# Windowed attention and a folded gated FFN in one kernel: attention by blocks of 128 queries, a new order of the work

## The chip, the core and the metric

The kernel runs on one core of a Trainium2 chip. The metric is the time of one execution on the device in microseconds; several executions are timed and the median counts. Lower is better.

## The reference

For 4 batches of 8 heads, 768 positions and head size 64, attention with four sink keys and a window of 128; its output, with the heads side by side, is the input of a gated feed-forward part.

```python
scores = scale * np.matmul(q, k.transpose(0, 1, 3, 2))
keep = is_sink | in_window           # pos < 4, or 0 <= q_pos - k_pos < 128
a = softmax(np.where(keep, scores, -1e9))
x = np.matmul(a, v)                  # -> [3072, 512]
h = (x @ w1) * (x @ w2) @ w3         # 512 -> 1024 -> 1024
out = h @ w_out                      # 1024 -> 512
```

## The kernel before, in words

All matmuls are in bf16. Since nothing nonlinear stands between them, w3 and w_out are folded into one matrix `w3o` at the start (`fold_w3` transposes rows of w3, `fold_mm` multiplies them with w_out). So each batch has these stages.

- **Keys and queries.** `load_qkv` loads k, q and v of a block of 128 positions on POOL's queue, converting to bf16. For batches 0 and 1, PE transposes them (`transposes`, tile `tp`) and VectorE copies them to `kqT`; for batches 2 and 3, SP issues DMA transposes (`transposes_dma`, one for k and one for q of a block).
- **Scores.** A pair of heads r is two matmul chains on the two halves of PE's rows (64 each, the head size). A score unit fills one PSUM tile `sc`; ScalarE takes the exponential (`ex`), VectorE multiplies with the mask (`am`). Most units are made by `scores(b, r, t)`: one pair of heads, a tile t of 256 queries, so four units for each of the three tiles of a batch. The tiles (0, 0) and (0, 1) (`BLOCKS`) are made by `block_scores(b, j, r0, r1)`: a block j of 128 queries and two pairs of heads (all four for j = 0, which has no earlier block). The two PSUM buffers of `sc` allow two units in flight. The keys at the sink are done by `sink_scores` (tile `sp`).
- **Values.** `values` or `block_values` multiply `am` with v (tile `av`), VectorE divides by the sums (`rec`, `xn`). `xn` is transposed to `xT` by PE (tile `xt`) or, for batches 1 to 3, by DMA on SP's queue (`x_transposes_dma`).
- **Gates.** `gate` makes x @ w1 and x @ w2 for a chunk of 256 or 384 tokens (tile `pg`); ScalarE copies one, VectorE multiplies the other with it into `ab`.
- **Output.** `project` multiplies `ab` with `w3o` for 128 tokens (tile `po`); ScalarE copies to SBUF, and SP sends the 256 KB out.

The order on every engine is made at build time. Each piece of work is a `task` with a priority, with its stages (engine and an assumed duration), with what must be done before (`after`), which loads it needs (`loads`), and what must have been started before (`started`). `landings` works out when loads are assumed to arrive, and `plan` then goes through assumed time: PE takes the task that can start first, and among those that can start at once the one with the lowest number (`prio`, changed for single tasks by `nudge`). `paced` tasks, the scores, are also held until ScalarE's backlog is small and until a given time after the scores before (`PACE`). `lead` marks the first of two score units that are to follow each other on PE; it waits for two free PSUM buffers. The engines then run what the plan wrote down, each in its order, and semaphores alone decide when.

At the start, `raws` lists nine transfers of 512 KB of w3 and w_out in fp32 that SP issues at once; ScalarE, VectorE or both convert them (`cast`). POOL waits for the raw transfer with the number `hold` (a copy to `spent`) and then begins its own loads in the order `order`. Where PE would stand still in the first 40 us, `keep_busy` puts in dummy matmuls (tile `pz`).

Of the kernel before, what the change touches and what calls it, by code (L numbers as in the profile page):

```python
# [21 lines left out]
def kernel(  # L22
# [13 lines left out]
    nc = tc.nc  # L36
    FP32 = mybir.dt.float32
# [89 lines left out]
    def load(what, *i):  # L127
# [9 lines left out]
        else:  # L137
# [13 lines left out]
    nudge = {("g", 0, 2, 6, 0): -300, ("g", 1, 2, 4, 0): -1200, ("g", 0, 1, 3, 1): 60, ("fm", 6, 3): 1500}  # L151
# [94 lines left out]
    def segments(t):  # L246
        segs = [] if t == 0 else [(2 * t - 1, 2 * t, P, 0)]
        return segs + [(2 * t, 2 * t, 2 * P, P), (2 * t + 1, 2 * t + 1, P, 3 * P)]

    ams = {}  # L250

    def scores(b, r, t):
        c0 = P if t == 0 else 0
        sc = ps_sc.tile([P, 2, 512], FP32, tag="sc", name="sc")
        for i, (kb, qb, n, c) in enumerate(segments(t)):
            for e in range(2):
                hp = slice(64 * e, 64 * e + 64)
                nc.tensor.matmul(sc[:, e, c:c + n], kT[b][hp, r, kb * P:(kb + 1) * P],  # L258
                                 qT[b][hp, r, qb * P:qb * P + n],
                                 start=True, stop=True)  # L260
        yield
        ex = work.tile([P, 2, 512], BF16, tag="ex", name="ex")
        nc.scalar.activation(ex[:, :, c0:], sc[:, :, c0:], ACTF.Exp, scale=scale)  # L263
        yield
        am = work.tile([P, 2, 512], BF16, tag="am", bufs=4, name="am")
        mk = maskt[:, min(t, 1):min(t, 1) + 1, c0:].to_broadcast([P, 2, 512 - c0])
        nc.vector.tensor_mul(am[:, :, c0:], ex[:, :, c0:], mk)  # L267
        ams[b, r, t] = am
        yield
# [52 lines left out]
    def block_x_transposes(b, j):  # L322

        t, i = j // 2, j % 2
        xt = ps_mm.tile([P, NP, P], BF16, tag="mm", name="xt")
        for r in range(NP):
            nc.tensor.transpose(xt[:, r, :], xns[b, t][:, i, r, :, :].rearrange("p e d -> p (e d)"), ident)
        yield
        nc.scalar.copy(xT[b][:, :, j * P:(j + 1) * P], xt[:])
        yield  # L330

    def values(b, r, t):

        am = ams.pop((b, r, t))
        av = ps_mm.tile([P, 2, 2, D + 1], FP32, tag="mm", name="av")
        todo = []
        for i in range(2):
            if t > 0:
                q0 = (t - 1) * 256 + i * P
                todo.append((av[:, i, :, :].rearrange("p e d -> p (e d)"), es[b][:, q0:q0 + P],  # L340
                             vs[b][:, 2 * r:2 * r + 2, :].rearrange("p e d -> p (e d)")))
            for kb, c in ((2 * t + i - 1, 2 * i * P), (2 * t + i, (2 * i + 1) * P)):
                if kb >= 0:
                    for e in range(2):
                        todo.append((av[:, i, e, :], am[:, e, c:c + P],
                                     vN[b][:, kb, 2 * r + e, 0:D + 1]))
        for n, (o, lhs, rhs) in enumerate(todo):
            nc.tensor.matmul(o, lhs, rhs, start=(n == 0), stop=(n == len(todo) - 1),  # L348
                             skip_group_check=True)
        yield  # L350
        rec = work.tile([P, 2, 2, 1], FP32, tag="rec", name="rec")
        nc.vector.reciprocal(rec[:], av[:, :, :, D:D + 1])  # L352
        if r == 0:
            xns[b, t] = work.tile([P, 2, NP, 2, D], BF16, tag="xn", bufs=3, name="xn")
        nc.vector.tensor_mul(xns[b, t][:, :, r, :, :], av[:, :, :, 0:D],  # L355
                             rec[:].to_broadcast([P, 2, 2, D]))
        yield

    def x_transposes(b, r0, t):

        xt = ps_mm.tile([P, 2, 2, P], BF16, tag="mm", name="xt")
        for r in range(2):
            for i in range(2):
                nc.tensor.transpose(xt[:, r, i, :],
                                    xns[b, t][:, i, r0 + r, :, :].rearrange("p e d -> p (e d)"),
                                    ident)
        yield
        nc.scalar.copy(xT[b][:, r0:r0 + 2, t * 256:(t + 1) * 256],
                       xt[:].rearrange("p r i m -> p r (i m)"))
        yield  # L370
# [74 lines left out]
    def project(b, m, n0, n1):  # L445
# [10 lines left out]
        (nc.scalar if n0 > DM // 2 else nc.sync).dma_start(out=out[t0:t0 + P, n0:n1], in_=o_sb)  # L456
# [22 lines left out]
    def landings(taken, RAW=2.0, POOL=3.0, DGE=1.3, RAMP=(0.75, 1.0)):  # L479
# [3 lines left out]
        taken, owed = sorted((t + 4.0, us) for t, us in taken), 0.0  # L483
# [3 lines left out]
        while any(at[n] < len(q) for n, q in queues.items()):  # L487
# [8 lines left out]
            while taken and taken[0][0] <= now:  # L496
                owed += taken.pop(0)[1]
            if owed > 0.0:
                owed -= 0.02
                now += 0.02  # L500
                continue
# [3 lines left out]
            for n in busy:  # L505
# [35 lines left out]
    for i in range(KFF):  # L541
# [7 lines left out]
        for h, (j0, j1) in enumerate(FM[i]):  # L549
# [11 lines left out]
            if last and (i % 2 or i >= 4):  # L561
                tasks["fm", i, h]["frees"] = ("fm", i if i >= 4 else i - 1, 0)
    unit = []
    last_av = []
    for b in range(B):
        for t in range(NT):
# [17 lines left out]
            else:  # L584
                if b not in SINKS:
                    task(("ss", b, t), -1, sink_scores(b, t, t + 1), [("pe", 0.12), ("act", 0.4)],
                         qk + [("sk", b)], ring="mm", started=[] if (b, t) in BLOCKS else [("sc", b, 1, t)])
                elif t == 1:
                    more = [(n, b, kb) for n in (("tdk", "tdq") if (b, 2) in XPOSE else ("tpk",)) for kb in (4, 5)]
                    task(("ss", b, 1), -1, sink_scores(b, 1, NT), [("pe", 0.225), ("act", 0.6)],  # L590
                         qk + more + [("sk", b)], ring="mm", started=[("sc", b, 1, 1)])
            if (b, t) in BLOCKS:
                parts = [(j, r0, r0 + 2, [2 * i + r0 // 2]) for i, j in enumerate(kbs) for r0 in (0, 2)]
                if t == 0:
                    parts = [(0, 0, NP, [0, 1])] + parts[2:]
                for u, (j, r0, r1, avs) in enumerate(parts):
                    task(("sc", b, u, t), 4, block_scores(b, j, r0, r1),
                         [("pe", 0.23), ("act", 1.05), ("dve", 0.7)],
                         [("tpk", b, kb) for kb in (j - 1, j) if kb >= 0], ring="sc", paced=True,
                         started=([unit[-1][0]] if unit else []) + (unit[-4][1] if len(unit) > 3 else []))  # L600
                    for a in avs:
                        task(("av", b, a, t), 3, block_values(b, j, 2 * (a % 2)),
                             [("pe", 0.125 if j == 0 else 0.245 if j == 1 else 0.36), ("dve", 0.55)],
                             [("sc", b, u, t)] + ([("ss", b, 1 if b in SINKS else t), ("sv", b)] if t else []),
                             [("v", b, j)], "mm", last_av)
                        last_av = [("av", b, a, t)]
                    unit.append((("sc", b, u, t), [("av", b, a, t) for a in avs]))
                    if avs[-1] % 2:
                        task(("xt", b, 2 * (j % 2), t), 2.5, block_x_transposes(b, j),
                             [("pe", 0.225), ("act", 0.6)],  # L610
                             [("av", b, avs[-1] - 1, t), ("av", b, avs[-1], t)], [], "mm")
                continue
            for r in range(NP):
                after = list(qk)
                if b >= 2 and t == 0:
                    after += [("g", b - 2, len(CHUNKS[b - 2]) - 1, dt, 1) for dt in range(KFF)]
                lead = r % 2 == 0
                task(("sc", b, r, t), 4 if lead else 0, scores(b, r, t),
                     [("pe", 0.17), ("act", 0.83), ("dve", 0.58)] if t == 0 else
                     [("pe", 0.225), ("act", 1.05), ("dve", 0.7)], after, ring="sc",  # L620
                     slots=2 if lead else 1, paced=lead,
# [215 lines left out]
```

## Time and profile before

| | |
|---|---|
| timed runs | 196.29, 197.38, 197.56 us; median 197.38 |
| profiled execution | 196.08 us, of which the span of its instructions 194.4 us |
| PE, PEld busy | 188.2 and 123.7 us |
| VectorE, ScalarE, POOL busy | 114.4, 103.9 and 75.6 us |
| granted TensorE clock | 1.00 |
| DMA | 29.17 MB, mean 150 GB/s |

A busy time is the sum over an engine's instructions, and a share is that against the span. PE (the matmuls) and PEld (their weight loads) overlap each other. Matmuls are pipelined: the time from one start to the next is what a matmul costs in a row of them, not its own duration. The time of an execution has some 1.7 us around the span.

### The profile page before, as it was taken

The page shows a single profiled execution, that of the slowest core. Times are in us where ns is not written, and L with a number is a line of the kernel's source. Part 1 is how long each engine was busy: PE and PEld are TensorE (multiplying, and loading weights), DVE is VectorE, ACT ScalarE, POOL GpSimd, SP SyncE. Part 2 cuts the span into 40 slices and gives each one's busy share as a digit, 9 for nine tenths or more (in the row PEclk, how much of TensorE's full clock was granted, in tenths as well). Part 3 has the DMA queues.
Part 4 walks back from the last instruction along what each step waited for, and adds up shares of the span by engine and source line. Part 5 has one row for each costly group of instructions (what it writes and reads, how often), then busy time and mean ns, then how long its engine had stood idle before and what let it go on. Part 6 is the DMA issues. An engine that isn't in the chain of part 4 may idle for free.

```text
span 194.4 us, 4625 instructions
## 1 busy us (share of the span) xinstructions
PE 188.2 (97%) x1830; PEld 123.7 (64%) x1830; DVE 114.4 (59%) x277; ACT 103.9 (53%) x177; POOL 75.6 (39%) x102
## 2 busy tenths in 40 slices
PE   7899799999999999999999999999999999999993
PEld 2346376998867786788788455556666666644443
DVE  5465588755699987967678036778886434410000
ACT  3515369743866876566574376567773333333232
POOL 5199967689999944433364330000000000000000
PEclk9999999999999999999999999999999999999999
DMA  5999999999999999999999999999320200014334
GB/s 209 414 380 159 184 165 197 193 158 154 156 152 192 198 146 125 154 157 187 118 154 142 142 157 220 211 217 120 78 56 2 55 0 0 0 55 164 146 133 153
DMA packets 107589, 29.17 MB, mean 150 GB/s; under 512 B 98608, under 2 KB 103088, under 8 KB 107568
## 3 DMA queue, kind: packets, MB, share of 16 engines
q0 software_dynamic: 79520, 12.33, 90.5%
q1 hardware_dynamic: 27904, 16.49, 40.1%
q8 instruction: 14, 0.23, 0.5%
q10 hardware_dynamic: 144, 0.07, 0.1%
q14 instruction: 7, 0.06, 0.1%
HBM read 29.39 MB, written 6.29 MB: 184 GB/s over the span
## 4 chain that ended last, share of the span: by engine, by line
PE 82%; DMA 11%; POOL 3%; SPq 2%; issue 0%; DVE 0%; ACT 0%; DVEq 0%
PE pg L388 39%; PE po L449 21%; PE av L348 6%; PE sc L258 5%; DMA kqT<-qN 4%; DMA ab<-in_moe_w_dram 4%; DMA qN<-in_q_dram 3%; PE tp L211 3%; PE pw L435 2%; PE av L311 1%; PE sc L279 1%; SPq L375 1%; PE ph L435 1%; SPq L163 1%; PE sp L240 1%; POOL qN L108 1%
## 5 line engine op out<-in xcount | busy, mean ns | idle before, releaser
L388 PE MATMUL pg<-xT,w_sb 128*128 128x256 bf16 (+1 forms) x640 | 91.0, 294 | 0.0
L388 PEld LDWEIGHTS <-w_sb 128*128 128x128 bf16 x640 | 59.5, 98 | 20.1 <-issue 1.1
L395 ACT COPY a_sb<-pg 128x256 f32<-128x256 f32 (+1 forms) x80 | 33.3, 416 | 37.0 <-PE pg L388 22.5
L392 DVE TENSOR_TENSOR ab<-a_sb,pg 128x256 bf16<-128x256 f32 (+1 forms) x80 | 37.7, 472 | 24.8 <-PE pg L388 22.8
L449 PE MATMUL po<-w3o,ab 128*128 128x512 bf16 (+2 forms) x208 | 43.0, 363 | 0.0
L263 ACT ACTIVATE ex<-sc 128x1024 bf16<-128x1024 f32 (+1 forms) x40 | 37.6, 962 | 6.5 <-PE sc L258 5.9
L449 PEld LDWEIGHTS <-ab 128*128 128x128 bf16 x208 | 19.3, 98 | 20.4 <-issue 0.2
L267 DVE TENSOR_TENSOR am<-ex,maskt 128x1024 bf16<-128x1024 bf16 (+1 forms) x40 | 25.3, 646 | 9.9 <-ACT ex L263 9.9
L453 ACT COPY w_sb<-po 128x512 f32<-128x512 f32 (+2 forms) x25 | 14.1, 566 | 25.9 <-PE po L449 25.8
L108 POOL DMA_DIRECT2D vN<-in_v_dram x24 | 21.6, 902 | 12.9 <-DMA kN<-in_k_dram 9.9
L108 POOL DMA_DIRECT2D qN<-in_q_dram x24 | 22.1, 919 | 9.9 <-DMA vN<-in_v_dram 6.2
L108 POOL DMA_DIRECT2D kN<-in_k_dram x24 | 22.0, 918 | 7.7 <-DMA qN<-in_q_dram 5.4
L355 DVE TENSOR_TENSOR xn<-av,rec 128x256 bf16<-128x256 f32 x40 | 17.0, 425 | 1.4
L348 PE MATMUL av<-vN,am 128*128 128x65 bf16 x296 | 16.7, 193 | 0.0
L348 PEld LDWEIGHTS <-am 128*128 128x128 bf16 x296 | 14.5, 97 | 1.8 <-DVE rec L352 0.2
L258 PE MATMUL sc<-kqT 64*128 64x128 bf16 (+1 forms) x216 | 11.8, 238 | 0.2 <-DMA kqT<-qN 0.2
L453 DVE COPY w_sb<-po 128x128 f32<-128x128 f32 x1 | 0.3, 292 | 19.7 <-ACT w_sb L453 19.7
L348 PE MATMUL av<-vs,es 128*128 128x130 bf16 x56 | 11.0, 220 | 0.0
L213 DVE COPY kqT<-tp 128x1024 bf16<-128x1024 bf16 x12 | 8.3, 689 | 4.6 <-PE tp L211 4.4
L352 DVE RECIPROCAL rec<-av 128x4 f32<-128x4 f32 x40 | 7.1, 178 | 5.9 <-PE av L348 5.5
L258 PEld LDWEIGHTS <-kqT 64*128 64x128 bf16 x216 | 7.0, 94 | 4.6 <-issue 4.0
L283 ACT ACTIVATE ex<-sc 128x1024 bf16<-128x1024 f32 x7 | 7.2, 1026 | 4.2 <-PE sc L279 4.2
(71 smaller groups left out, 140.5 us busy)
## 6 DMA issues: line engine op xcount, KB each, us to landing
out_dram<-w_sb SPq DMA_DIRECT2D x23, 256.0 KB
kN<-in_k_dram POOLq DMA_DIRECT2D x24, 128.0 KB, 8.4
qN<-in_q_dram POOLq DMA_DIRECT2D x24, 128.0 KB, 8.2
vN<-in_v_dram POOLq DMA_DIRECT2D x24, 128.0 KB, 8.0
w_sb<-in_moe_w_dram POOLq DMA_DIRECT2D x9, 256.0 KB, 8.3
ab<-in_moe_w_out_dram SPq DMA_DIRECT2D x3, 512.0 KB
ab<-in_moe_w_dram SPq DMA_DIRECT2D x3, 512.0 KB
kN<-in_moe_w_out_dram SPq DMA_DIRECT2D x1, 512.0 KB
```

What stands on the lines that cost most here:

```text
L108: nc.gpsimd.dma_start(out=dst, in_=rows(src, b, kb))
L213: nc.vector.tensor_copy(kqT[b][:, :, :, kb * P:(kb + 1) * P], tp[:])
L258: nc.tensor.matmul(sc[:, e, c:c + n], kT[b][hp, r, kb * P:(kb + 1) * P], qT[b][hp, r, qb * P:qb * P + n], start=True, stop=True)
L263: nc.scalar.activation(ex[:, :, c0:], sc[:, :, c0:], ACTF.Exp, scale=scale)
L267: nc.vector.tensor_mul(am[:, :, c0:], ex[:, :, c0:], mk)
L348: nc.tensor.matmul(o, lhs, rhs, start=(n == 0), stop=(n == len(todo) - 1), skip_group_check=True)
L355: nc.vector.tensor_mul(xns[b, t][:, :, r, :, :], av[:, :, :, 0:D], rec[:].to_broadcast([P, 2, 2, D]))
L388: nc.tensor.matmul(pg[:], w_sb[:, kk, dt * P:(dt + 1) * P], xT[b][:, kk, tk], start=(kk == 0), stop=(kk == NP - 1))
L392: nc.vector.tensor_mul(ab[b][:, dt, tk], gate_a.pop((b, c, dt))[:], pg[:])
L395: nc.scalar.copy(a_sb[:], pg[:])
L449: nc.tensor.matmul(po[:], ab[b][:, kk, m * P:(m + 1) * P], w3o[:, kk, n0:n1], start=(kk == 0), stop=(kk == KFF - 1))
L453: (nc.vector.tensor_copy if n0 == DM // 2 else nc.scalar.copy)(o_sb, po[:])
```

## The change

Every batch is now done by `block_scores` and `block_values`; `scores`, `values`, `x_transposes`, `segments` and `BLOCKS` are gone. `UNITS` lists all 44 score units in order of batch and block (one for block 0 of a batch, two for each later one). They are paired one after the other along this list, also across blocks and batches, except those in `SINGLE`. A unit waits for the transposed keys of its own blocks (`keys`), the leading one for those of its partner too, no longer for a whole tile. DMA transposes of `xn` are tasks for each block, when its own values are done.

The raw transfers come in another order and are converted by other engines, and POOL waits for the fourth of them (`hold = 4`). `landings` no longer takes the transposes' share away piece by piece, but assumes 2.1 us in place of 0.845 for a load from block 2 of batch 2 on, and a delay that grows; a DMA transpose is assumed to be done after 9.2, 6.0 or 3.0 us, not 8.4, 5.0 or 2.7. `nudge` and `PACE` hold other numbers, the sinks' priority is 0.5 and not -1. Three output tiles (`HALVED`) are sent as two DMAs each.

```diff
-    BLOCKS = ((0, 0), (0, 1))
+    UNITS = [(b, j, r0, NP if j == 0 else r0 + 2) for b in range(B) for j in range(NB) for r0 in ((0,) if j == 0 else (0, 2))]
+    SINGLE = ((0, 0), (3, 0))
+    HALVED = ((3, 1), (3, 2), (3, 3))
...
-    raws = [("wo", 2, 4, "act"), ("w3", 4, 5, "act"), ("w3", 0, 1, "both"), ("wo", 0, 2, "dve"),
-            ("w3", 1, 2, "dve"), ("wo", 4, 6, "dve"), ("wo", 6, 8, "dve"), ("w3", 2, 3, "both"),
-            ("w3", 3, 4, "act")]
-    hold = 5
+    raws = [("wo", 0, 2, "dve"), ("w3", 0, 1, "dve"), ("w3", 4, 5, "dve"), ("wo", 2, 4, "act"),
+            ("w3", 2, 3, "both"), ("w3", 3, 4, "act"), ("wo", 4, 6, "both"), ("wo", 6, 8, "act"),
+            ("w3", 1, 2, "act")]
+    hold = 4
...
-    nudge = {("g", 0, 2, 6, 0): -300, ("g", 1, 2, 4, 0): -1200, ("g", 0, 1, 3, 1): 60, ("fm", 6, 3): 1500}
+    nudge = {("g", 0, 1, 2, 0): -300, ("g", 1, 0, 2, 1): 60, ("p", 3, 5, 256): -60, ("av", 3, 1, 1): 1500,
+             ("tpk", 1, 5): 3, ("g", 1, 0, 2, 0): -60, ("xt", 0, 0, 2): -3, ("g", 1, 1, 0, 1): 60}
...
-        (nc.scalar if n0 > DM // 2 else nc.sync).dma_start(out=out[t0:t0 + P, n0:n1], in_=o_sb)
+        step = DM // 2 if (b, m) in HALVED else n1 - n0
+        for c in range(n0, n1, step):
+            (nc.scalar if n0 > DM // 2 else nc.sync).dma_start(out=out[t0:t0 + P, c:c + step],
+                                                               in_=o_sb[:, c - n0:c - n0 + step])
...
-            return [(0.95 if i[0] == 0 else 0.87, 0.845, [(x, i[0], kb)])
+            return [(0.95 if i[0] == 0 else 0.87, 0.845 if 6 * i[0] + kb < 14 else 2.1, [(x, i[0], kb)])
...
-                        arrive[key] = now + lag + min(2.5, max(0.0, 0.25 * (now - 36.0)))
+                        arrive[key] = now + lag + min(2.5, max(0.0, 0.25 * (now - 36.0))) + min(3.0, max(0.0, 0.1 * (now - 70.0)))
...
+    roles, partner, lead = {}, {}, None
+    for n, (b, j, r0, _) in enumerate(UNITS):
+        if lead is None and (b, j) not in SINGLE and n + 1 < len(UNITS):
+            roles[b, j, r0], partner[b, j, r0] = "lead", UNITS[n + 1][:2]
+            lead = b, j, r0
+        else:
+            roles[b, j, r0] = "more" if lead else "single"
+            lead = None
...
+                after = keys(b, j) + (keys(*partner[b, j, r0]) if role == "lead" else [])
...
+                if avs[-1] % 2:
+                    both = [("av", b, 2 * i, t), ("av", b, 2 * i + 1, t)]
+                    if (b, t) in X_XPOSE:
+                        task(("xd", b, t, i), 1, x_transposes_dma(b, t, i), [("sp", 1.3), ("dma", 1.2)], both)
...
-    PACE = [[0, 1.3, 0], [0, 0, 0], [6.2, 0, 0], [5.3, 0, 0]]
+    PACE = [[0, 0, 0], [5.8, 3.9, 0], [0, 0, 0], [0, 0, 0]]
...
-                    done[k["name"]] = at + (8.4 if at < end - 4.0 else 5.0 if at < end else 2.7)
+                    done[k["name"]] = at + (9.2 if at < end - 4.0 else 6.0 if at < end else 3.0)
```

How the order changes is seen at three places.

**PE, scores of block 1 of batch 0**, before (L279 is `block_scores`, L435 `fold_mm`, L311 `block_values`):

```order
L435 MATMUL ph_296<-wo_sb_81,w3t_354 128x512
L279 LDWEIGHTS kqT_0_95
L279 MATMUL sc_380<-kqT_0_95 128x128
...
L311 MATMUL av_393<-vN_0_91,am_375 128x65
...
L405 MATMUL tp3_409<-ident_73,w3_sb_80 128x128
...
L279 MATMUL sc_418<-kqT_0_95 128x128
```
and now (L259 is `block_scores`, L291 `block_values`, L345 `fold_w3`):

```order
L291 MATMUL av_389<-vN_0_91,am_377 128x65
L259 LDWEIGHTS kqT_0_95
L259 MATMUL sc_395<-kqT_0_95 128x128
...
L259 MATMUL sc_408<-kqT_0_95 128x128
...
L345 LDWEIGHTS w3_sb_80
L345 MATMUL tp3_419<-ident_73,w3_sb_80 128x128
```
Two units of eight matmuls (`sc_380`, `sc_418`) stood apart, with folds and values between them; now the two (`sc_395`, `sc_408`) follow each other without anything between.

**SP, the transposes of batch 2's last blocks** (`kqT_2`, L218, of loaded k and q) among those of `xn` (L375), before:

```order
L218 DMA_TRANSPOSE kqT_2_97<-kN_2_89 128x4x128
L375 DMA_TRANSPOSE xT_1_100<-xn_1528 128x4x128 x2
L218 DMA_TRANSPOSE kqT_2_97<-qN_2_85 128x4x128
...
L375 DMA_TRANSPOSE xT_2_101<-xn_1685 128x4x128 x2
...
L218 DMA_TRANSPOSE kqT_3_98<-kN_3_90 128x4x128
```
and now (L221 and L315):

```order
L315 DMA_TRANSPOSE xT_1_100<-xn_1540 128x4x128
L315 DMA_TRANSPOSE xT_2_101<-xn_1709 128x4x128
L221 DMA_TRANSPOSE kqT_2_97<-kN_2_89 128x4x128
L221 DMA_TRANSPOSE kqT_2_97<-qN_2_85 128x4x128
...
L315 DMA_TRANSPOSE xT_2_101<-xn_1709 128x4x128
L221 DMA_TRANSPOSE kqT_2_97<-qN_2_85 128x4x128
L315 DMA_TRANSPOSE xT_2_101<-xn_1958 128x4x128
```
The transposes of `xn` stood in twos, and both halves of a tile went when the tile's last values were done. Now they stand singly among those of k and q. The last row but one is q of block 5 of batch 2; ahead of it stands the `xT` transpose of block 1 of that batch.

**VectorE, the start**, before (L410 copies transposed rows of w3, L415 converts raw weights):

```order
L410 COPY kN_1_88<-tp3_203 128x512
L410 COPY kN_1_88<-tp3_208 128x512
L415 CAST w3_sb_80<-ab_0_103 128x512
L415 CAST wo_sb_81<-ab_1_104 128x1024
L410 COPY w3t_231<-tp3_220 128x512
```
and now (L350 and L355):

```order
L355 CAST wo_sb_81<-ab_0_103 128x1024
L355 CAST w3_sb_80<-ab_0_103 128x1024
L350 COPY w3t_212<-tp3_202 128x512
L350 COPY w3t_212<-tp3_207 128x512
L355 CAST w3_sb_80<-ab_0_103 128x1024
L350 COPY kN_1_88<-tp3_223 128x512
```
The first two raw transfers were converted by ScalarE before; now the first three are converted by VectorE, and the first rows that PE transposes come from its second conversion.

More of the change, by code (lines that the diff above doesn't have):

```diff
@@ L244, in sink_scores @@
         yield
-    def segments(t):
-        segs = [] if t == 0 else [(2 * t - 1, 2 * t, P, 0)]
-        return segs + [(2 * t, 2 * t, 2 * P, P), (2 * t + 1, 2 * t + 1, P, 3 * P)]
     ams = {}
[L252 to L269, printed above, removed]
     def block_scores(b, j, r0, r1):
@@ L329, in block_x_transposes @@
         nc.scalar.copy(xT[b][:, :, j * P:(j + 1) * P], xt[:])
[L330 to L369, printed above, removed]
         yield
@@ L591 @@
                          qk + more + [("sk", b)], ring="mm", started=[("sc", b, 1, 1)])
[L592 to L612, printed above, removed]
@@ L613 @@
[L613 to L614 removed]
+            for b_, j, r0, r1 in UNITS:
+                if (b_, j // 2) != (b, t):
+                    continue
+                u, i = (j % 2) * 2 + r0 // 2 - (j == 1), j % 2
+                avs = [0, 1] if j == 0 else [2 * i + r0 // 2]
+                role = roles[b, j, r0]
+                after = keys(b, j) + (keys(*partner[b, j, r0]) if role == "lead" else [])
                 if b >= 2 and t == 0:
                     after += [("g", b - 2, len(CHUNKS[b - 2]) - 1, dt, 1) for dt in range(KFF)]
[L617 to L621, printed above, removed]
[L622 to L632 removed]
@@ L633 @@
-            if (b, t) in X_XPOSE:
-                for i in range(2):
-                    task(("xd", b, t, i), 1, x_transposes_dma(b, t, i), [("sp", 1.3), ("dma", 1.2)],
-                         [("av", b, NP - 1, t)])
+                task(("sc", b, u, t), 0 if role == "more" else 4, block_scores(b, j, r0, r1),
+                     [("pe", 0.23), ("act", 1.05), ("dve", 0.7)], after, ring="sc",
+                     slots=2 if role == "lead" else 1, paced=role != "more",
+                     started=([unit[-1][0]] if unit else [])
+                     + (unit[-3 if role == "lead" else -4][1] if len(unit) > 3 else []))
@@ new lines @@
+                for a in avs:
+                    task(("av", b, a, t), 3, block_values(b, j, 2 * (a % 2)),
+                         [("pe", 0.125 if j == 0 else 0.245 if j == 1 else 0.36), ("dve", 0.55)],
+                         [("sc", b, u, t)] + ([("ss", b, 1 if b in SINKS else t), ("sv", b)] if t else []),
+                         [("v", b, j)], "mm", last_av)
+                    last_av = [("av", b, a, t)]
+                unit.append((("sc", b, u, t), [("av", b, a, t) for a in avs]))
@@ L796, in plan @@
             advance(k, free[e])
-        return taken
-    taken = []
-    for last in (False, False, True):
-        landings(taken)
-        taken = plan(last)
+    landings()
+    plan(True)
 _INS = ['q', 'k', 'v', 'n_sink', 'window', 'moe_w1', 'moe_w2', 'moe_w3', 'moe_w_out']
```

35 lines of the change are left out of this document (10 added, 25 removed).

## The prediction

> **What bounds the kernel now.** I read the page first, then PE's own waits, then the chain of waits at the two places where PE stood still, then SP's and POOL's queues there.
>
> ```profile
> span 194.4 us, 4625 instructions
> PE 188.2 (97%) x1830; PEld 123.7 (64%) x1830; DVE 114.4 (59%) x277; ACT 103.9 (53%) x177; POOL 75.6 (39%) x102
> PE 82%; DMA 11%; POOL 3%; SPq 2%; issue 0%; DVE 0%; ACT 0%; DVEq 0%
> ```
> TensorE is busy 97% of the span, ScalarE and VectorE little over half. The chain that ends last is PE for 82%, and a transfer for 11%. So a change gains by taking work off PE or by ending one of PE's waits. These are PE's waits, all of them:
>
> ```profile
> PE pz L463 <- DVE ksbd L172: 1.3, 1, 1.3
> PE tp L211 <- DMA qN<-in_q_dram: 1.1, 1, 1.1
> PE tp L405 <- DVE w_sb L415: 0.5, 1, 0.5
> PE sc L258 <- DMA kqT<-qN: 0.2, 1, 0.2
> ```
> Beside the start (1.3 us, and dummy matmuls that cover the first raw weights), PE waits 1.8 us in all. Nothing that shortens ScalarE's or VectorE's work is worth anything by itself. The longest, 1.1 us, is for q of block 1 of batch 0:
>
> ```profile
> 15.42 6.64 DMA qN<-in_q_dram
> 22.11 0.40 PE L211 MATMUL tp<-ident,qN 128*128 128x128 bf16 x4 [1.10 <-DMA qN<-in_q_dram]
> 26.94 0.39 PE L211 MATMUL tp<-ident,kN 128*128 128x128 bf16 x4
> 27.16 0.39 PE L211 MATMUL tp<-ident,qN 128*128 128x128 bf16 x4
> 179.68 11.64 PE L449 MATMUL po<-w3o,ab 128*128 128x512 bf16 x69
> ```
> That load landed at 15.42 + 6.64 = 22.06. PE ends at 179.68 + 11.64 = 191.3. From block 2's q transposes (27.16) to there are 164.2 us, in which PE idles for 0.2. Up to 27 us the loads set the pace, behind it PE's own work does.
>
> ```profile
> 9.00:14.80 5.80, 5.80 (x41) 2.96 (x38) 3.94 (x9) 0.62 (x1) 5.01 (x7) 1.00 1.04 376
> 16.00:20.00 4.00, 4.00 (x41) 2.34 (x40) 2.22 (x6) 1.81 (x3) 4.00 (x6) 1.00 2.42 159
> ```
> In these stretches (length, PE, PEld, DVE, ACT, POOL, granted clock, DMA share, GB/s) the DMA engines have no idle time, first with raw weights at 376 GB/s, then with q, k, v in short runs at 159. The granted clock is 1.00 throughout.
>
> **The change part by part.** PE's matmul columns stay the same: a tile unit of batch 0 to 3 had 4 or 6 matmuls of 128 or 256 columns, a block unit has 8 of 128. In columns, 136 x 128 + 80 x 256 + 56 x 128 = 45,056 before and 352 x 128 = 45,056 now. Values, gates, folds and projections are the same in number. What changes is how often PE goes into the 64-row shape of the scores and out of it.
>
> ```profile
> 22.77 0.59 PE L435 MATMUL pw<-wo_sb,qN 128*128 128x512 bf16 x2
> 23.20 0.59 PE L435 MATMUL ph<-wo_sb,w3t 128*128 128x512 bf16 x2
> 23.73 0.40 PE L279 MATMUL sc<-kqT 64*128 64x128 bf16 x8
> 24.06 0.60 PE L435 MATMUL ph<-wo_sb,w3t 128*128 128x512 bf16 x2
> 63.31 0.62 PE L258 MATMUL sc<-kqT 64*128 64x128 bf16 x12
> 63.86 0.35 PE L348 MATMUL av<-vN,am 128*128 128x65 bf16 x6
> ```
> Starts tell the pace. Two matmuls of 512 columns take 23.20 - 22.77 = 0.43; the same two ahead of a score run take 0.53, so the way in costs 0.10. A block unit alone takes 24.06 - 23.73 = 0.33, a pair of tile units (12 matmuls) 0.55; the second unit of a pair thus adds 0.22, and the way out costs 0.11. A turn in and out is 0.21. The order has 27 score runs before (20 pairs of tile units, 7 block units singly) and 23 now (21 pairs, two singles): 4 turns, 0.84 us, of which one lies ahead of block 2's transposes and three behind it. The bounds are two turns and four, 0.4 and 0.84, since two runs next to a sink unit may keep part of a turn.
>
> That more and smaller matmuls cost nothing in themselves is in the same rows: 8 of 128 columns cost 0.33 - 0.11 = 0.22, as do the 6 wider ones of a tile unit. The Trainium skill speaks against it ("TensorE: Matmul & The Clock Gate", Back-to-back issue gap): in a stream of weight load and matmul pairs it gives some 81 ns a matmul at 128 columns. By that, as an estimate, the 80 added matmuls would cost 6.5 us and the forecast would be a loss; the trace's 0.33 us for 8 with their weight loads does not agree.
>
> ScalarE and VectorE hardly notice:
>
> ```profile
> L263 ACT ACTIVATE ex<-sc 128x1024 bf16<-128x1024 f32 x28 | 28.2, 1026 | 4.6 <-PE sc L258 4.0 <-DVE rec L352 0.5
> L263 ACT ACTIVATE ex<-sc 128x768 bf16<-128x768 f32 x12 | 9.4, 812 | 2.0 <-PE sc L258 1.9
> L283 ACT ACTIVATE ex<-sc 128x1024 bf16<-128x1024 f32 x7 | 7.2, 1026 | 4.2 <-PE sc L279 4.2
> ```
> 44 exponentials at 1026 ns are 45.1 us against 28.2 + 9.4 + 7.2 = 44.8; the 0.3 lies under PE, with ScalarE at 53%. Without that cover it would cost its 0.3. The masks change as little (44 at 686 ns are 30.2 us).
>
> ```profile
> L267 DVE TENSOR_TENSOR am<-ex,maskt 128x1024 bf16<-128x1024 bf16 x28 | 18.9, 686 | 8.4 <-ACT ex L263 8.4
> 63.17 0.33 SPq L456 DMA_DIRECT2D out_dram<-w_sb  x1
> 172.94 18.81 SPq L456 DMA_DIRECT2D out_dram<-w_sb  x13
> ```
> The pieces of the halved tiles go out from SP, 0.33 us an issue, three more issues in a queue that has 13 in 18.8 us there; what follows the last matmul (191.3 to 194.4) is the same quarter tile as before. Both are costed at nothing.
>
> **The start.** The raw row that lands second, the first to be folded, is now cast by VectorE.
>
> ```profile
> 5.92 1.04 ACT L415 CAST w_sb<-ab 128x1024 bf16<-128x1024 f32 x1 [0.21 <-DMA ab<-in_moe_w_dram]
> 7.03 0.62 PE L405 MATMUL tp<-ident,w_sb 128*128 128x128 bf16 x8
> 9.77 0.69 DVE L415 CAST w_sb<-ab 128x1024 bf16<-128x1024 f32 x1
> 9.79 0.71 POOL L201 COPY spent<-ab 128x1 f32<-128x1 f32 x1 [4.38 <-DMA ab<-in_moe_w_dram]
> 18.74 0.94 POOL L108 DMA_DIRECT2D qN<-in_q_dram  x1
> qN<-in_q_dram POOLq DMA_DIRECT2D x24, 128.0 KB, 8.2
> ```
> A cast of 0.69 in place of 1.04 starts PE at about 6.7, not 7.03. That 0.35 is only lent: PE then meets block 2's q, issued at 18.74 and with the median 8.2 there at 26.9. POOL now waits for the fourth raw transfer, not the fifth, and so starts one transfer earlier (512 KB at 376 GB/s, 1.4 us). If loads were held by POOL, they would all land 1.4 earlier; since the DMA engines have no idle time from 9 to 20, an earlier load only takes its share from the raw weights. I take nothing for it, and keep 1.4 as the bound of a gain and 0.7 (half of it, if the mixture slows the raw weights that PE folds) as that of a loss. PE then runs block 2's q transposes at about 27.05, 0.1 earlier.
>
> **Batch 2's keys.** The wait of 0.2 at 95 should go, and new ones may come. A pair of blocks now asks for its transposed q and k when its turn comes, while a tile asked for two blocks at once, later for the second half of the batch.
>
> ```profile
> 87.58 7.72 DMA kqT<-qN
> 95.34 0.56 PE L258 MATMUL sc<-kqT 64*128 64x256 bf16 x10 [0.17 <-DMA kqT<-qN]
> 90.83 1.25 SPq L218 DMA_TRANSPOSE kqT<-qN  x1
> 95.97 2.51 SPq L375 DMA_TRANSPOSE xT<-xn  x2
> 99.94 1.68 SPq L218 DMA_TRANSPOSE kqT<-qN  x1
> 111.29 0.62 PE L258 MATMUL sc<-kqT 64*128 64x128 bf16 x12
> 74.02 0.87 POOL L108 DMA_DIRECT2D qN<-in_q_dram  x1 [0.45 <-DMA vN<-in_v_dram]
> DMA to landing us min/median/max: 5.6/8.2/21.2
> ```
> Before, blocks 4 and 5 were wanted at 111.29, 80.1 us ahead of PE's end. In the new order, 168 projection and 272 gate matmuls with 180,224 columns stand from block 5's scores on (at 512 columns in 0.216: 76.0 us), 13 score units (2.9), seven turns (1.5), 144 value matmuls at some 0.034 (4.9) and two sink units (0.7): 86 us. From block 4's on there are 91, with 36 gate matmuls of 256 columns more. With PE's end at 190.4 they are wanted at 99.4 and 104.4. A transpose lands 7.72 after its issue. Block 4's q, issued at 90.83 as before, would be there at 98.6: in time by 0.8. Block 5's, issued as before at 99.94, would come at 107.7, 3.3 too late. But its load (issued 74.02, the longest landing 21.2) is there by 95.2, and it stood on SP behind two xT transposes that start at 95.97; now one goes ahead of it, for values that PE, by the same count of work, computes at about 90. Issued at 95.2, it lands by 102.9, 1.5 us in time. I take no new wait; the bound is 3.3.
>
> **Sum.** 0.1 at the front, 3 x 0.21 = 0.63 in turns behind it, 0.2 for the wait at 95: 0.9 us. The profiled execution has 196.08 (its span 194.4 and 1.7 around it), so 195.2. The three timed runs (196.29, 197.38, 197.56) and the profiled one differ by 1.5, with a mean of 196.8; a run of the changed kernel I put at 196.8 - 0.9 = 195.9, which is 0.75% under the median shown. What a measurement of this kernel can tell from no change is about 1%.
>
> **Rivals.** First, a larger gain: POOL's earlier start does bring the loads earlier by one transfer, 1.4 us. For it speaks that PE meets a late load at 22.11 and again near 27; against it the DMA share in the windows. 195.9 - 1.4 = 194.5. Second, a loss: SP holds block 5's keys of batch 2 (and 4's, 0.8 from it) behind an xT transpose that waits for values; if SP issues block 5's q after 96.7, PE waits in order with gates and projections queued behind the scores, at worst 3.3 us, and 0.4 more where block 4 is late too: 195.9 + 3.7 = 199.6, slower than before. For it speaks that PE already waited 0.2 at 95 for the same kind of transfer, that 90.83 to 95.97 shows SP standing behind xT; against it the 1.5 us worked out. Third, small matmuls do cost: if each of the 80 added ones took the 55 ns that a 128-column transpose takes (4 in 0.22 from 26.94 to 27.16), 4.4 us more: 200.3. Against it are the rows of 0.33 and 0.55. It is the mechanism of the rule of the Trainium skill that is weighed above. Fourth, the new order gives its turns back in small waits and nothing changes: 196.8.
>
> **How the numbers follow.** Forecast 0.46, larger gain 0.22, late keys 0.20, small matmuls 0.03, nothing 0.09. Faster by over 1% means under 195.4: most of the larger gain (0.20) and the lower third of the forecast (0.17), 0.37. Slower by over 1% means over 199.4: two thirds of the late keys, the small matmuls and some of what none of these names, 0.22. Within 1%: 0.41. The range from 194.2 to 199.2 holds the larger gain, the forecast and the smaller half of the late keys; the forecast's own is 195.0 to 196.9.
>
> **What would show it.** Right: PE's first fold at about 6.7, block 2's q transposes near 27.0, 23 score runs, about 163.5 us from those transposes to PE's end, no wait of sc for kqT. Wrong: tp of block 1 or 2 well before its time of now (the loads do come earlier), a wait of sc for kqT between 83 and 105, a run of 16 score matmuls over 0.55, or PE waiting for am or for a weight's cast.

## The result, and the profile after

The changed kernel takes 197.76 us (median of 22 runs, 196.38 to 199.57), the kernel before 196.55 (22 runs): a ratio of 1.0059, 95% interval 1.0037 to 1.0081. A small loss, where 0.75% of gain was forecast. The page of the profiled execution after the change has these lines:

```profile
span 195.3 us, 4782 instructions
PE 188.3 (96%) x1908; PEld 125.0 (64%) x1908; DVE 114.1 (58%) x273; ACT 105.0 (54%) x175; POOL 75.4 (39%) x102
PE 66%; DMA 22%; POOL 5%; SPq 2%; DVE 1%; issue 1%; ACT 0%; DVEq 0%
```
PE's busy time hardly changed (it has 78 more matmuls, the scores alone 80 more), the span grew by 0.9. The chain that ends last is now PE for 66%, not 82%, and a transfer for 22%, not 11%. A transfer counts in this chain with its whole flight, however short the wait for it was: of the 22%, 11% is one load of w1 and w2, 8% are transposes to `kqT`. What they cost is in PE's waits (engine, tile, line, who released it; us in total, times, longest; the 1.3 us at the very start, the same as before, and 0.2 for a cast are not shown):

```profile
PE ph L375 <- DVE w3t L350: 0.5, 2, 0.3
PE sp L243 <- DMA kqT<-qN: 0.5, 1, 0.5
PE tp L345 <- DVE w_sb L355: 0.4, 2, 0.3
PE sc L259 <- DMA kqT<-qN: 0.3, 1, 0.3
PE pg L328 <- DMA w_sb<-in_moe_w_dram: 0.2, 1, 0.2
```
The wait of 1.1 for q of block 1 is gone, as is the single one of 0.2 for `kqT`. In their place stand small waits at two places. The first is the start, in VectorE's timeline and then in PE's:

```profile
21.57 0.70 DVE L234 TENSOR_TENSOR vs<-vc,ones_s 128x512 bf16<-128x512 f32 x1 [1.23 <-DMA vc<-in_v_dram]
22.18 0.42 DVE L350 COPY w3t<-tp 128x512 bf16<-128x512 bf16 x1
```
```profile
6.39 0.62 PE L345 MATMUL tp<-ident,w_sb 128*128 128x128 bf16 x8 [0.16 <-DVE w_sb L355]
22.65 0.60 PE L375 MATMUL ph<-wo_sb,w3t 128*128 128x512 bf16 x2 [0.21 <-DVE w3t L350]
27.43 0.39 PE L214 MATMUL tp<-ident,qN 128*128 128x128 bf16 x4
```
The first fold starts at 6.39 (7.03 before), yet block 2's q transposes at 27.43 (27.16 before). VectorE waits for `vc`, the sinks' values, and the copy of `w3t` behind it keeps PE. The second place is 84 to 107:

```profile
84.48 0.62 PE L259 MATMUL sc<-kqT 64*128 64x128 bf16 x16 [0.28 <-DMA kqT<-qN]
91.55 3.22 PE L328 MATMUL pg<-xT,w_sb 128*128 128x256 bf16 x28
95.27 0.29 PE L243 MATMUL sp<-kqT,ksbd 128*32 128x256 bf16 x4 [0.50 <-DMA kqT<-qN]
100.85 0.62 PE L259 MATMUL sc<-kqT 64*128 64x128 bf16 x16
106.02 0.29 PE L243 MATMUL sp<-kqT,ksbd 128*32 128x256 bf16 x4
```
PE waits ahead of each of blocks 1, 3, 4 and 5 of batch 2. Starts give the whole price: 28 gate matmuls at 0.109 from 91.55 end at 94.60, so `sp` at 95.27 is 0.67 late, 0.10 of it the way into another shape. In the same way 0.35, 0.57, 0.13 and 0.21 come out, and 0.32 at 41 for a load of w1 and w2 (it landed at 41.53, before at 40.80): 1.58 us in all. All but this last are waits for batch 2's q, and SP's queue shows why they come late (start, duration):

```profile
82.70 2.09 SPq L315 DMA_TRANSPOSE xT<-xn  x1
84.88 2.00 SPq L221 DMA_TRANSPOSE kqT<-kN  x1
86.97 1.29 SPq L221 DMA_TRANSPOSE kqT<-qN  x1
88.36 2.97 SPq L315 DMA_TRANSPOSE xT<-xn  x2
91.41 1.34 SPq L221 DMA_TRANSPOSE kqT<-kN  x1
92.85 2.17 SPq L221 DMA_TRANSPOSE kqT<-qN  x1
95.11 1.28 SPq L221 DMA_TRANSPOSE kqT<-kN  x1
96.48 1.48 SPq L315 DMA_TRANSPOSE xT<-xn  x1
98.05 1.27 SPq L221 DMA_TRANSPOSE kqT<-qN  x1
```
One issue follows the other without a pause (from 63 to 106), some 1.6 us each; before, SP stood idle from 92.1 to 95.97. The chain of waits gives what follows the q issues of blocks 3 and 5:

```profile
86.97 8.25 DMA kqT<-qN
98.05 7.92 DMA kqT<-qN
```
They release PE at 95.2 and 106.0.

### The profile page after: what moved, and what is told of

Its sections match the earlier page's. It is cut to its first block, busy times and chain, and to the rows that moved or that the text cites. A ratio compares the mean times of both kernels' runs of the same rounds, so it can differ in the third digit from the quotient of the medians.

```text
span 195.3 us, 4782 instructions
## 1 busy us (share of the span) xinstructions
PE 188.3 (96%) x1908; PEld 125.0 (64%) x1908; DVE 114.1 (58%) x273; ACT 105.0 (54%) x175; POOL 75.4 (39%) x102
## 4 chain that ended last, share of the span: by engine, by line
PE 66%; DMA 22%; POOL 5%; SPq 2%; DVE 1%; issue 1%; ACT 0%; DVEq 0%
PE pg L328 32%; PE po L389 21%; DMA w_sb<-in_moe_w_dram 11%; DMA kqT<-qN 8%; PE av L291 5%; PE sc L259 4%; DMA ab<-in_moe_w_out_dram 4%; POOL w_sb L113 2%; PE tp L214 2%; SPq L221 1%; POOL qN L110 1%; POOL vN L110 1%; PE sp L243 1%; POOL kN L110 1%; SPq L166 1%
## 5 line engine op out<-in xcount | busy, mean ns | idle before, releaser
L263 ACT ACTIVATE ex<-sc 128x1024 bf16<-128x1024 f32 x44 | 44.5, 1026 | 6.8 <-PE sc L259 5.5
L267 DVE TENSOR_TENSOR am<-ex,maskt 128x1024 bf16<-128x1024 bf16 x44 | 29.7, 685 | 4.7 <-ACT ex L263 4.4
L298 DVE TENSOR_TENSOR xn<-av,rec 128x256 bf16<-128x256 f32 x48 | 20.4, 424 | 1.7
L291 PE MATMUL av<-vN,am 128*128 128x65 bf16 x352 | 18.7, 193 | 0.0
L291 PEld LDWEIGHTS <-am 128*128 128x128 bf16 x352 | 16.7, 97 | 2.2
L295 DVE RECIPROCAL rec<-av 128x4 f32<-128x4 f32 x48 | 8.5, 178 | 16.3 <-PE av L291 16.2
L259 PE MATMUL sc<-kqT 64*128 64x128 bf16 x352 | 13.8, 217 | 0.3 <-DMA kqT<-qN 0.3
L259 PEld LDWEIGHTS <-kqT 64*128 64x128 bf16 x352 | 10.0, 94 | 3.7 <-issue 2.6
L291 PE MATMUL av<-vs,es 128*128 128x130 bf16 x64 | 12.3, 220 | 0.0
L375 PE MATMUL ph<-wo_sb,w3t 128*128 128x512 bf16 x32 | 8.7, 380 | 0.9 <-DVE w3t L350 0.5
L406 PE MATMUL pz<-ksbd 128*128 128x512 bf16 x16 | 6.3, 541 | 1.3 <-DVE ksbd L175 1.3
```

Of the source, the lines that this page charges most:

```text
L259: nc.tensor.matmul(sc[:, e, r - r0, s, :], kT[b][hp, r, kb * P:(kb + 1) * P], qT[b][hp, r, j * P:(j + 1) * P], start=True, stop=True)
L263: nc.scalar.activation(ex[:], sc[:].rearrange("p e r s q -> p e (r s q)"), ACTF.Exp, scale=scale)
L267: nc.vector.tensor_mul(am[:].rearrange("p e (r x) -> p (e r) x", x=n), ex[:].rearrange("p e (r x) -> p (e r) x", x=n), maskt[:, v:v + 1, c ...
L298: nc.vector.tensor_mul(xns[b, t][:, i, r0:r0 + 2, :, :], av[:, :, :, 0:D], rec[:].to_broadcast([P, 2, 2, D]))
L375: nc.tensor.matmul(po, w3T[i][:, j, :], wo_sb[:, j, :], start=(j == 0), stop=(j == KFF - 1))
```

## The experiments

In those that move single steps, the order that the planner wrote for the changed kernel is kept, and a step is put ahead of another one in that list (`move`). Each was compared with runs of the kernel before on the same chip. "Sinks later" and the two with both cures ran on another chip than the rest; the changed kernel itself, run again beside these three, came out as in the first measurement:

> The changed kernel once more, every order as it is, beside the next three and against the same runs of the kernel before: a ratio of 1.006 to 1.010, and in its profile once more waits for kqT of 1 to 3.4 us between 83 and 107 and VectorE waiting 0.9 to 2.4 us for vc at 20 to 23.

It took 197.98 us, ratio 1.0063 (1.0029 to 1.0098).

**What one turn is worth.** Ten pairs of score units are pulled apart.

```diff
+    move(("pe", ("sc", 2, 1, 1)), ("pe", ("g", 1, 1, 3, 0)))   # and nine more
```


> The changed kernel, but in ten of its pairs of score units the second unit goes one gate or projection task later on PE (33 score runs, not 23); nothing else is moved. The prediction's price of a turn, 0.21 us, gives +2.1 us: ratio 1.0166, about 199.9 us. Rival 'turns are free' (the loss is that the removed turns were worth nothing): ratio 1.006 as the changed kernel. Rival 'half a turn' (0.1 us): 1.011.

199.02 us, ratio 1.0154 (1.0121 to 1.0188). The turns cost what the prediction said. In the table, the net time is that from block 2's q transposes to the start of PE's last matmul, less the waits for transfers in between (worked out from starts as above; "sinks later" with 0.43 for `am`; the 0.78 of "both cures" is three delays, each too short for the list of waits: 0.20 at 28.67 for q of block 3, 0.29 at 40.37 for w1 and w2, 0.28 at 88.08 for `ab`):

| kernel | block 2's q | last matmul | waits | net |
|---|---|---|---|---|
| before | 27.16 | 191.11 | 0.27 | 163.68 |
| changed | 27.43 | 192.13 | 1.58 | 163.12 |
| changed, once more | 28.67 | 193.26 | 1.47 | 163.12 |
| hold five | 27.83 | 192.90 | 1.96 | 163.11 |
| whole tiles | 27.71 | 193.80 | 2.98 | 163.11 |
| keys first | 27.61 | 191.91 | 1.20 | 163.10 |
| sinks later | 26.46 | 192.13 | 2.55 | 163.12 |
| ten pairs split | 27.47 | 194.14 | 1.43 | 165.24 |
| slow SP | 28.66 | 191.89 | 0.00 | 163.23 |
| both cures | 26.02 | 190.04 | 0.78 | 163.24 |

Six executions with the changed order on PE agree within 0.02 us in the net time. The ten splits add 2.12, 0.21 a turn; the change saved 0.56. All that differs otherwise is when block 2's q comes and the waits, from 1.2 to 3.0 us by execution.

**SP's order.**

```diff
+    move(("sp", ("tdq", 2, 1)), ("sp", ("xd", 1, 1, 0)))
+    move(("sp", ("tdk", 2, 3)), ("sp", ("p", 0, 4)))
+    move(("sp", ("tdq", 2, 3)), ("sp", ("p", 0, 4)))
+    move(("sp", ("xd", 2, 0, 0)), ("sp", ("xd", 2, 0, 1)))
+    move(("sp", ("tdq", 2, 5)), ("sp", ("xd", 2, 0, 1)))
```


> The changed kernel with five moves in SP's order alone, PE's order untouched: batch 2's q of block 1 is transposed ahead of an xT transpose, k and q of block 3 ahead of an output tile and an xT transpose, and q of block 5 ahead of an xT transpose (two xT transposes of batch 2 thus go later). Theory 'SP': the keys are late because they stand behind other work in SP's queue. Then they land 1.5 to 2.6 us earlier, PE's waits at 84, 95, 101 and 106 (0.35 + 0.57 + 0.2 + 0.2 = 1.3 us) go, and the ratio to the kernel before falls from 1.006 to about 0.999 (196.4 us). Rival 'load': the transposes land late because the DMA engines are taken by the loads; then the landings and the ratio (1.006) stay. Rival 'hidden': an xT transpose that goes later makes a gate wait instead; then the waits for kqT go and PE waits of pg for xT come, and the ratio stays.

196.57 us, ratio 1.0026 (0.9999 to 1.0053): between what theory SP and its rivals gave. PE's waits show that the cure only went half the way:

```profile
PE sc L259 <- DMA kqT<-qN: 1.1, 2, 0.6
```
The waits at 84, 95 and 106 are gone, so the order of SP's queue does set when these keys land; left are block 4 (0.66 at 100.3) and a new one for the first block of batch 3 (0.54 at 113.3). No gate waits for `xT`. What is pushed back in a queue without pauses is late next.

**Another queue.**

```diff
-        nc.sync.dma_start_transpose(
+        (nc.scalar if src is qN[2] and kb else nc.sync).dma_start_transpose(
```


> The changed kernel, each step at its place, but the five DMA transposes of batch 2's q of blocks 1 to 5 are issued by ScalarE's queue and not by SP's. The transposes and the loads on the DMA engines stay the same. Theory 'SP's rate': SP issues without a pause from 63 to 106, some 1.6 us a transpose, and batch 2's keys are late because they queue there. Then SP has some 8 us to spare, PE's waits for kqT between 83 and 115 (1.4 to 3.4 us in the profiles so far) go but for 0.3, and the ratio falls to 0.998 (between 0.996 and 1.001), though ScalarE loses some 1.3 us at each issue. Rival 'DMA': the transposes take 8 to 9 us to land because they share the DMA engines with the loads, and come late from any queue: waits and ratio (1.006 to 1.010) stay. Rival 'ScalarE': the exponentials now stand behind the issues and PE waits for am instead: ratio 1.005 or more, with PE waits of av for am.

228.2 us, ratio 1.1597 (1.1532 to 1.1663). None of the three foresaw it (the rival 'ScalarE' has the side, but PE waited for ScalarE's copies of gates and outputs, not for `am`): ScalarE stood still at each issue (its timeline, two rows that follow each other and one later).

```profile
83.32 1.28 ACTq L221 DMA_TRANSPOSE kqT<-qN  x1
84.70 0.37 ACT L335 COPY a_sb<-pg 128x256 f32<-128x256 f32 x1 [10.76 <-DMA kN<-in_k_dram]
...
98.23 0.58 ACT L393 COPY w_sb<-po 128x512 f32<-128x512 f32 x1 [9.71 <-issue]
```
It stood 4 to 9 us ahead of four of the five issues (the row names one semaphore of a list; the one that came last, at 83.1, is that of a transpose which SP issued at 75.44). As built, each transpose on ScalarE waits until the transposes on SP have landed, and the next on SP for that one. The Trainium skill ("DMA: Bandwidth & Descriptors", Silent corruption: two transposing streams in flight at once) says that it must be so, since transposes of two queues in flight together can corrupt each other; no run here shows the corruption, only the waits. They are not the whole price: PE stood still for 9.0, 6.7, 4.7 and 3.7 us, 24 in all, and from 76 to 130 its granted clock was 0.66 to 0.81, where it is 1.00 in the changed kernel; its busy time grew from 188.3 to 196.1, by 8. So this run says nothing on SP's rate, and a second queue was no way out.

**The loads beside the transposes.** Batch 3's k, q and v are not loaded; it computes with batch 1's tiles, so its part of the output is another.

```diff
+    qN[3], kN[3], vN[3] = qN[1], kN[1], vN[1]
...
+                if i[0] < 3:
                     load_qkv(i[0], kb)
```


> The changed kernel without the loads of batch 3's k, q and v (18 transfers, 2.4 MB out of the stretch from 74 to 130); batch 3 computes with batch 1's tiles instead, with the same instructions in the same order. Theory 'SP's rate' in its pure form (SP needs 1.3 to 1.7 us an issue whatever the DMA engines do): SP's issues keep their mean of 1.6 us from 80 to 106 and PE's waits for kqT stay over 1. Rival 'DMA': without the loads an issue takes 1.25, a transpose lands in under 5 us, and the waits for kqT of blocks 3 to 5 are gone.

One run, 197.01 us. SP's timeline:

```profile
87.73 3.02 SPq L317 DMA_TRANSPOSE xT<-xn  x2
90.84 1.30 SPq L223 DMA_TRANSPOSE kqT<-kN  x1
92.23 3.17 SPq L223 DMA_TRANSPOSE kqT<-qN  x1
...
101.28 1.22 SPq L223 DMA_TRANSPOSE kqT<-kN  x1
102.55 1.25 SPq L223 DMA_TRANSPOSE kqT<-qN  x1
103.92 1.19 SPq L317 DMA_TRANSPOSE xT<-xn  x1
```
From 83 to 95, while batch 2's own loads still ran (the last landed at 98.5), an issue took 1.68 us on average and a transpose landed after 8.2; from 95 to 106 they took 1.29 and 3.4 (means of 7 and 8 in the records). Block 5's q, issued at 98.20, was there at 102.08, where the changed kernel's, issued at 98.05, took 7.92. The waits for blocks 4 and 5 are gone; those for blocks 1 and 3, which fall while loads still run, stay (0.3, and 1.3 at 95.6), so 'DMA' missed on block 3, and the waits as a whole are no less. On what makes a transpose slow 'DMA' is right, and SP's pace goes with it. The Trainium skill ("DMA: Bandwidth & Descriptors", Issuing engines are not separate DMA queues) has SP's and POOL's transfers interleave on the same 16 engines; the trace agrees, with 7.92 beside the loads and 3.88 without.

**Asking later.** The planner is told that a transpose holds SP longer.

```diff
-                    ... transposes_dma(src, dst, kb), [("sp", 1.4), ("dma", 1.2)],
+                    ... transposes_dma(src, dst, kb), [("sp", 1.75), ("dma", 1.2)],
-                    ... x_transposes_dma(b, t, i), [("sp", 1.3), ("dma", 1.2)], both)
+                    ... x_transposes_dma(b, t, i), [("sp", 1.65), ("dma", 1.2)], both)
```


> The changed kernel with two numbers of the planner: a DMA transpose is assumed to hold SP for 1.75 (keys) or 1.65 us (xn), not 1.4 or 1.3. The order is the same up to 61 us; behind it batch 2's scores are asked for later, with gates and projections ahead of them, and the runs of scores stay 23. Theory 'asked too early' (SP's rate, not foreseen by the planner): the waits for kqT go but for 0.5, PE's net work stays at 162.7 us from block 2's q transposes, and the ratio falls to 0.997 to 1.001. Rival 'nothing to fill with': gates that are drawn forward wait for xT, or batch 3's keys become late in their place: ratio 1.005 or more.

195.90 us, ratio 0.9994 (0.9963 to 1.0025). Not one wait for `kqT` is left. The late start of this execution, with block 2's q at 28.66, does not explain it: the changed kernel's second profile has it at 28.67 and waits 1.47 us. Batch 2's scores stand behind more gates, and there was enough to fill with; the net time is that of the changed kernel within 0.1 (163.23, not the 162.7 that was expected).

**The start.** POOL waits for the fifth raw transfer again.

```diff
-        nc.gpsimd.tensor_copy(spent[:], casts[hold - 1][1][:, 0:1])
+        nc.gpsimd.tensor_copy(spent[:], casts[hold][1][:, 0:1])
```


> The changed kernel, every engine's order untouched, but POOL waits for the fifth raw transfer and not the fourth, so its first load is issued some 1.2 us later. Theory 'front': POOL's earlier start slowed the last two raw transfers (16.7 against 14.8 before) and thereby PE's folds; then these land about 1 us earlier, block 2's q transposes return from 27.4 to about 27.2, and the ratio falls by 0.001 to 0.002 to about 1.004. Rival 'raw order': it is the new order of the raw transfers and casts; then PE's folds keep their small gaps and the ratio stays at 1.006, or rises by 0.001 where the later first loads cost something.

198.06 us, ratio 1.0092 (1.0058 to 1.0126): nothing won. The ninth raw transfer did land earlier, at 15.84 (16.69 in the changed kernel), but the first row of w3 on POOL's queue later, at 17.11 (16.14), and PE met that:

```profile
17.15 0.40 PE L345 MATMUL tp<-ident,w_sb 128*128 128x128 bf16 x4 [1.01 <-DMA w_sb<-in_moe_w_dram]
```
And VectorE no longer waited for `vc`, which led to the chain behind it. Of the eight small loads of `vc` on SP, each goes out when a raw transfer has landed, the last with the ninth. The last three, in the kernel before and in the changed one:

```profile
12.32 2.79 SPq L199 DMA_DIRECT2D vc<-in_v_dram  x3
```
```profile
12.95 4.00 SPq L202 DMA_DIRECT2D vc<-in_v_dram  x3
```
They are out at 15.11 and 16.95. Before, the copy that needs them stood ready at 19.25 and waited for nothing; now it waits 0.7 to 2.4 us in every profile in which it has its old place, except with hold five and with the old raw order:

> The changed kernel with the nine raw transfers, their converting engines and the hold of the kernel before. The planner makes a new order from it, so its time is not compared; the stretch up to 30 us is read from the profile. If the new order of the raw transfers is what makes the start late, block 2's q transposes stand at 27.2 or earlier (27.4 to 27.8 in the changed kernel and its variants). If the block pairs or chance are, they stay at 27.5.

There, block 2's q stood at 27.57 without a wait for `vc`, but its third raw transfer came late, at 8.16 (7.18 before, 7.83 in the changed kernel; see the last section). So the old raw order is no cure by itself, and what the new one costs at the start is not settled by this run. The new order was bad behind it (two runs, ratio 1.0204; `kqT` 1.5 and `xT` 1.3 us late).

Then the copy itself was moved.

```diff
+    move(("dve", ("sv", 0)), ("dve", ("av", 0, 2, 0)))
```


> The changed kernel with one step of VectorE moved: the product of the sinks' values of batch 0 (vs from vc), needed by values from about 31 us on, goes behind the copies of w3t and kqT, not ahead of them. Theory 'vc' for the start: the last vc load is issued when the ninth raw transfer has landed (16.7, before 14.9), VectorE waits for it, and the copy of w3t behind it lets PE wait 0.4 to 1.5 us at 22 to 24. Then this wait goes and block 2's q transposes stand at 27.2 or earlier. Theory 'keys bound' for the rest: batch 2's keys come when the loads and SP let them, so PE, being earlier, waits that much longer for kqT between 83 and 107: the ratio stays within 0.002 of the changed kernel's (1.006 to 1.010). Rival 'the parts add up': the ratio falls by 0.003 to 0.005 below it.

197.10 us, ratio 1.0048 (1.0020 to 1.0077). By the medians it is 0.9 us under the changed kernel beside it, by the ratios 0.0015, with intervals that overlap: whether this cure gains alone stays open. Block 2's q comes at 26.46, and in the profile that lead is lost again, as 'keys bound' said:

```profile
26.46 0.39 PE L214 MATMUL tp<-ident,qN 128*128 128x128 bf16 x4
```
```profile
PE sp L243 <- DMA kqT<-qN: 1.9, 2, 1.2
```
In its profile the last matmul starts at 192.13, exactly where it does in the changed kernel's. This is one profile, and the waits vary without a cure too ("whole tiles" waits 2.98 from a start at 27.71), so it does not show that such a lead must be lost.

Nor is the lead all the cure's. The third raw transfer landed at 6.94 here and at 7.83 in the changed kernel's profile; from there to block 2's q it is 19.52 and 19.60 us. Three profiles in which it landed alike, at 8.11 to 8.12, tell what the cure is worth: with the copy at its old place block 2's q stood at 28.67 ("changed, once more") and 28.66 ("slow SP"), with the copy moved at 27.18 (the variant of both cures, below). That is 1.5 us, where VectorE had waited 2.3 us for `vc`; where it waited 1.2, as in the first profile, the gain is smaller.

**Both cures**, and a variant with transposes assumed to land later (10.5, not 9.2):

> Both cures: a transpose is assumed to hold SP for 1.75 and 1.65 us, so batch 2's scores come later in the order, and the sinks' values of batch 0 go later on VectorE. In the kernel with the first cure alone PE had no wait for kqT and block 2's q transposes stood at 28.66, 1.2 us later than in the changed kernel. If both causes are the right ones: block 2's q at 27.3, waits for kqT under 0.5, PE's end at 190.4 to 190.8, ratio 0.993 to 0.996, faster than both kernels. Rival 'keys bound' here too: the order's slack is under 1 us, the waits come back, ratio 0.999 to 1.002.

> As the kernel with both cures, and a transpose of the middle stretch is also assumed to land after 10.5, not 9.2 us. If the kernel with both cures still waits for kqT, this one waits less: ratio 0.993 to 0.996. If that one has no wait, this one gains nothing more, and may lose 0.001 to 0.003 where gates run out ahead of batch 3's scores.

195.26 us, ratio 0.9953 (0.9926 to 0.9980), and 195.42, 0.9954 (0.9928 to 0.9979). These are all the waits of PE with both cures:

```profile
PE pz L406 <- DVE ksbd L175: 1.3, 1, 1.3
PE ph L375 <- DVE w3t L350: 0.3, 1, 0.3
PE tp L345 <- DVE w_sb L355: 0.2, 1, 0.2
```
The block order with both cures is faster than the kernel before, by 0.5%, and than the changed one; the variant adds nothing, since no wait for `kqT` was left. The profile of the first has an early start (block 2's q at 26.02, not the 27.3 expected) from an early third raw transfer (6.69); the times are medians of 12 runs each.

**Halved output tiles.**

```diff
-    HALVED = ((3, 1), (3, 2), (3, 3))
+    HALVED = ()
```


> The changed kernel with the three output tiles sent whole again, orders untouched but for three DMA issues fewer on SP. The prediction costed the halves at nothing: the ratio stays at 1.006 within 0.001. Rival 'tail': each further issue delays the last output, 3 x 0.33 us at most: ratio 1.001.

198.48 us, ratio 1.0117 (1.0078 to 1.0156). From the start of the last matmul to the end of the span it is 3.34 us, in the changed kernel 3.16, before 3.24: the tail explains 0.2 at most. The rest is in the waits for `kqT`, 2.98 in this profile; the interval meets that of the changed kernel (up to 1.0098), and whether the halves help a little stays open.

## Why the prediction was wrong

- **Turns: right.** 0.63 us were forecast behind block 2's transposes, 0.56 came (163.68 - 163.12), and a turn costs 0.21. Small matmuls cost nothing that shows: with 80 more of them the net time fell by nearly the three turns, and the third rival's 4.4 us did not come.
- **Batch 2's keys: the step that failed.** The sum had -0.2 here: the wait at 95 was to vanish and none to come. The profiles of the changed order show waits for keys of 1.3 to 3.0 us, against 0.27 before. The wait at 95 was for block 3's q, whose issue hardly moved (86.97, before 87.58), so nothing took it away. "A transpose lands 7.72 after its issue" was somewhat short (7.9 to 8.3 for blocks 3 to 5, 9.5 for block 1); what failed were the issue times. I worked out blocks 4 and 5 only, and took block 5's q to go out at 95.2, as soon as it was loaded. SP was then at block 5's k (95.11), then an `xT` transpose (96.48), and came to it at 98.05. Block 1 and block 3, which I had not looked at, gave the larger waits. I priced each transpose by its landing, not the queue by its pace: 1.6 us an issue, with no pause left once blocks 4 and 5 are wanted some 10 and 5 us earlier than before (at 100.7 and 105.8, not 111.3). The second rival (late keys, 0.20) came nearest: block 5's q did go out after 96.7. But the `xT` transpose ahead of it did not stand waiting for values, SP was behind with its issues, and blocks 4 and 5, the only ones that the rival names, make up 0.34 of the 1.26 us.
- **The start: later, not earlier.** Block 2's q at 27.05 was forecast; with the copy of the sinks' values at its place it came at 27.3 to 28.7. The early fold was, as said, only lent, and the loads did not come earlier, as said: that of block 2's q landed at 27.05. But I had PE meet this load, and it met VectorE first: the last raw transfers slowed down beside POOL's earlier loads (from the third landing to the ninth 8.9 us, with hold five 7.9), `vc` went out behind them, and VectorE, waiting for it, held up `w3t`. "ScalarE and VectorE hardly notice" was read from their shares; the order in VectorE's queue was not looked at. Of the 0.27 us by which the profile is late, how much the change made is open: its third raw transfer landed 0.65 later than before, and it did so with the old raw order too.
- **The rest.** ScalarE's side and the tail were as forecast. The sum by its terms for the profiled execution: -0.56 for turns, +0.27 at the start, +1.31 for waits (1.58 - 0.27; 0.32 of it is the load of w1 and w2), is +1.02, as PE's last matmul shows (192.13 - 191.11).

## What to carry to other kernels

When an order asks for something earlier, work out the pace of the queue that delivers it over the whole stretch, not the latency of one transfer: in a queue without pauses, what is moved forward makes something else late, and the engine that asks waits. Asking later, with other work in between, took these waits away at next to no cost (0.1 us). An engine at 58% can still hold the critical one through a single step in its queue that waits for a small load. And before an earlier start is credited to a change, look whether the first transfers landed alike: here they shift the start by up to 1 us, the cure by 1.5 at most.

## What the runs showed of the hardware

- A DMA transpose of 128 x 512 took 7 to 10 us to land beside loads in short runs, and 2.4 to 3.9 us from 98 to 118 us once these were gone; its issue on SP shrank from 1.68 to 1.29 us with it.
- Five transposes on a second queue cost 32 us: 24 of PE's waits, and 8 while the granted clock was 0.66 to 0.81.
- The third raw transfer landed at 6.7 to 7.2 in three profiles and at 7.65 to 8.3 in the others, with nine transfers of the same size ahead of everything else (between 5 and 6 us 311 GB/s in the changed kernel's profile, 406 in that of the kernel before). That moves the start by up to 1 us from execution to execution, and what causes it stays open.
